# Weight loads of a fused linear-attention and MLP kernel issued from ScalarE's queue instead of SyncE's

## The chip, the cores and the metric

The kernel runs on one core of one Trainium2 chip. Its metric is the device time of one execution in microseconds. Before the change five runs gave a median of 189.07 us (188.53 to 190.00).

A core has TensorE (PE in the profile; its weight loads are PEld), VectorE (DVE), ScalarE (ACT), GpSimd (POOL) and SyncE (SP). Transfers between the chip's main memory and a core's memory are carried by 16 DMA engines. An instruction on SP, ACT or POOL issues such a transfer; "SPq" and "ACTq" in the profile are those engines' instruction streams as far as they issue or wait.

## What is computed

A gated linear attention over 4 batches, 8 heads, 768 steps and head size 48, and then an MLP with SiLU on its 3072 x 384 result:

```python
f = 1.0 / (1.0 + np.exp(-f_logit))
state = np.zeros((B, H, D, D), dtype=np.float32)
for t in range(S):
    state = f[:, :, t, :, None] * state + np.einsum('bhd,bhe->bhde', k[:, :, t], v[:, :, t])
    y[:, :, t] = np.einsum('bhd,bhde->bhe', q[:, :, t], state)
x = y.transpose(0, 2, 1, 3).reshape(B * S, H * D)
h = x @ w_in                       # 384 x 2048
g = h * (1.0 / (1.0 + np.exp(-h)))
out = g @ w_out                    # 2048 x 384
```

All inputs and the output are float32 in main memory. The products run in bfloat16.

## The kernel before

The sequence is cut into 6 chunks of 128 steps; a chunk of one batch is a **unit**, so there are 24 units (unit u has chunk u // 4 and batch u % 4). Two neighbouring units are a pair. For one unit the kernel does the following:

- SP loads f, k, q and v (L485). Units 0 to 3 are loaded singly (192 KB each tensor), the later ones by pairs (384 KB). Each tensor has five tiles that hold a pair each.
- ACT takes an exponential of f (L492) and a logarithm of one plus it (L494). TensorE sums the logs over the chunk with a triangular matrix (`cs`, L565 and L569). ACT takes three exponentials of the sums (`ia` L572, `a` L574, `al` L576).
- POOL multiplies k (L578) and copies v to bfloat16 (L580); DVE multiplies q (L582). TensorE transposes both (`tq`, L588), DVE copies the result out (L590), TensorE makes the scores (`sc`, L599), DVE masks them (L603), TensorE makes the unit's y (L608, L612), DVE casts it (L616), and it is transposed into `xT` (L620, L622). The state is carried on by TensorE (L630), DVE (L635, L637) and POOL (L641). From unit 12 on, the DMA transpose of SP does the first transposition (L592), from unit 15 also the second (L625).
- The MLP: TensorE multiplies by w_in (L529 for units 0 to 5, singly; L540 by pairs) into three PSUM tiles `mlp`, ACT applies SiLU (L526, L536) into `hT`, TensorE multiplies by w_out (L551), DVE copies the result out (L554 to L559) and POOL or SP stores it (L562).

ACT needs one function table for the exponentials and logarithms and another for SiLU. It changes between them with a table load (L677).

**The weights.** w_in and w_out come in four pieces of 768 KB each. A piece is read as float32 into a staging tile and cast to bfloat16 into a tile that stays (L520 on POOL and DVE, L519 on ACT). There are four staging tiles `ws` for w_in (128 x 3 x 512) and two, `wt`, for w_out (128 x 4 x 384), so pieces 3 and 2 of w_out reuse the tiles of pieces 1 and 0 and wait for their casts. The order of the reads is w_in 1, 2, w_out 1, w_in 3, 0, w_out 0, 3, 2. Casts: w_in 0, 1, 2 and w_out 0, 3 on POOL, w_in 3 and w_out 1 on DVE, w_out 2 on ACT. All eight reads are issued by SP among the loads of f, k, q and v (L505, L510).

**The order.** No scheduler on the chip decides anything. A planner in the same file (`make_tasks`, `schedule`, `planned`) gives each task an engine, a duration and a priority, plays the program through with a model of the engines and of the DMA queue, and hands back all tasks sorted by their planned start. `emit` is then called for each in this order, and every engine runs its instructions in the order in which they were emitted. An instruction that has to wait holds up all later ones of its engine. The framework adds the waits that the data demand. It also gives each DMA one of eight semaphores; a DMA's issue waits until the previous DMA with its semaphore has landed.

Before 60 us of planned time, TensorE's idle stretches are filled with products of a blank tile (`warm`, L652).

Of the kernel before, what the change touches and what calls it, by code (L numbers as in the profile page):

```python
# [414 lines left out]
def kernel(  # L415
# [10 lines left out]
    nc = tc.nc  # L426
# [4 lines left out]
    d_model, d_ff = moe_w_in.shape  # L431
# [14 lines left out]
        ws=([128, KT, d_ff // CFG["w_pieces"][0]], F32), wt=([128, NT // CFG["w_pieces"][1], d_model], F32),  # L446
# [12 lines left out]
    NI, NO = CFG["w_pieces"]  # L459
    w_in_sb = [sb.tile([128, KT, d_ff // NI], BF16, name=f"w_in{n}") for n in range(NI)]  # L460
    w_out_sb = [sb.tile([128, NT // NO, d_model], BF16, name=f"w_out{n}") for n in range(NO)]
    w_in_src = moe_w_in.rearrange("(ko ki) n -> ki ko n", ki=128)
# [12 lines left out]
    where = {}  # L475
    for t in tasks:
        for x in t.acq + t.use:
            where[x.key] = buf[x.cls, x.slot]
    at = lambda *key: where[key]

    def load(x, us):
# [14 lines left out]
    def emit(t):  # L496
# [5 lines left out]
        if kind == "wi":  # L502
            w = d_ff // NI
            n = rest[0] * w
            return nc.sync.dma_start(out=at("ws", rest[0]), in_=w_in_src[:, :, n:n + w])  # L505
        if kind == "wo":
            m, w = rest[0], NT // NO
            src = moe_w_out[m * w * 128:(m + 1) * w * 128].rearrange("(m p r) d -> p m r d", p=128, r=4)
            dst = at("wt", m).rearrange("p (m r) d -> p m r d", r=4)
            return nc.sync.dma_start(out=dst[:, 0] if w == 4 else dst, in_=src[:, 0] if w == 4 else src)  # L510
        if kind in ("ci", "co"):
            j, N = rest[0], NI if kind == "ci" else NO
            n, i = divmod(j, 4 // N)
            if kind == "ci":
                dst, src = w_in_sb[n][:, :, 512 * i:512 * i + 512], at("ws", n)[:, :, 512 * i:512 * i + 512]
            else:
                dst, src = w_out_sb[n][:, 4 * i:4 * i + 4, :], at("wt", n)[:, 4 * i:4 * i + 4, :]
# [14 lines left out]
        if kind in ("mi", "si"):  # L532
# [4 lines left out]
            for i in range(2):  # L537
                n = 2 * j + i
# [52 lines left out]
        elif kind == "qkD":  # L591
            nc.sync.dma_start_transpose(out=at("qkT", u).rearrange("p j n c -> p (j n) c"),  # L592
                                        in_=at("qk", u).rearrange("p j h d -> p (j h d)"))
# [60 lines left out]
    with tc.manual_schedule():  # L654
        nc.scalar.preload_act_table_set(SETS[mode])
        blank = sb.tile([C, C], BF16, name="blank")
        nc.vector.memset(blank, 0.0)  # L657
        first = [t for t in tasks if t.eng == "SP"][:4]
        for t in first:
            emit(t)  # L660
        make_upper_triangular(nc, triu, 1.0, diag=True)
        nc.vector.memset(ones, 1.0)
        for cls in ("lf", "qk"):
            for s in range(SLOTS[cls]):
                nc.vector.memset(buf[cls, s][:, :, :, D:64], 0.0)
        make_identity(nc, ident)
        for b in range(B):
            nc.vector.memset(buf[f"st{b}", 0], 0.0)
        acts = [t for t in tasks if t.mode]
        after = {a.idx: b.mode for a, b in zip(acts, acts[1:]) if b.mode != a.mode}  # L670
        for t in tasks:
            while idles and idles[0][0] <= t.start:
                warm(*idles.pop(0)[1:])
            if t not in first:
                emit(t)
            if t.idx in after:
                nc.scalar.preload_act_table_set(SETS[after[t.idx]])  # L677
# [30 lines left out]
```

## Time and profile before

| | us |
|---|---|
| median of five runs | 189.07 |
| the profiled execution | 189.16 |
| its span, first to last instruction | 187.40 |
| TensorE busy in the span | 173.4 |
| ACT busy | 131.2 |
| DVE busy | 95.8 |
| POOL busy | 69.8 |
| blank products (L652) within TensorE's time | 10.0 |

The 16 DMA engines move 34.2 MB, 31.8 MB of them on SP's queue, which takes 78.1% of the 16 engines' span. The TensorE clock was granted in full throughout. Of TensorE's 14.0 idle us, 9.0 lie in the first 30.2 us, 1.1 between 80 and 120 us and 3.8 in the last 9.

How to read it: a row of a timeline has the start, the length, the engine, the line, the operation, output and input tiles with their shapes, the number of instructions merged into the row, and in brackets the idle time of the engine before the row with what ended it. A digit in the row of slices is a tenth of busy time in one fortieth of the span. An engine's idle time matters only where the engine sets the pace.

### The profile page before, as it was taken

Reading aid. Unit: us, or ns where it says so; the run is one execution under the profiler, and the core shown is the slowest. Engines: PE = TensorE matmul, PEld = TensorE weight load, DVE = VectorE, ACT = ScalarE, POOL = GpSimd, SP = SyncE. Lnnn points to the kernel's source line nnn. Section 1 sums busy time; section 2 is a strip of 40 time slices with the busy share of each in tenths; the row PEclk is TensorE's granted clock in tenths of the full one; section 3 lists DMA queues with packets and bytes.
Section 4 is the critical chain, followed back from the end, with each engine's and each line's share of the span. In section 5 each row is a group of like instructions: output and inputs, shape, how many; then the busy total and the mean of one; then the engine's idle time right before and its main releaser. Section 6 shows DMA issues by size and latency. Waiting matters only on the chain.

```text
span 187.4 us, 4875 instructions
## 1 busy us (share of the span) xinstructions
PE 173.4 (93%) x2005; PEld 138.4 (74%) x2005; DVE 95.8 (51%) x185; ACT 131.2 (70%) x217; POOL 69.8 (37%) x112
## 2 busy tenths in 40 slices
PE   5986848999999999979999999999999999999991
PEld 4974747777878889768787787678688886966960
DVE  4287445444877773564627736875542415261011
ACT  4462734998797898998988788668669996810810
POOL 2347528444637470562751642490252006000000
PEclk9999999999999999999999999999999999999999
DMA  6999999899999998999998599478774866413101
GB/s 131 212 176 329 386 353 329 244 226 211 228 207 239 234 214 198 229 251 195 198 167 187 124 179 210 79 122 222 160 149 120 182 121 135 102 25 105 42 17 67
DMA packets 120389, 34.22 MB, mean 183 GB/s; under 512 B 116128, under 2 KB 117792, under 8 KB 120368
## 3 DMA queue, kind: packets, MB, share of 16 engines
q1 hardware_dynamic: 119664, 31.76, 78.1%
q0 software_dynamic: 704, 2.16, 3.3%
q8 instruction: 15, 0.25, 0.6%
q14 instruction: 6, 0.05, 0.1%
HBM read 25.17 MB, written 4.72 MB: 159 GB/s over the span
## 4 chain that ended last, share of the span: by engine, by line
PE 70%; SPq 11%; DMA 7%; ACT 5%; issue 2%; POOL 1%; DVE 1%; DVEq 0%; ACTq 0%
PE mlp L551 29%; PE mlp L540 24%; DMA q<-in_q_dram 7%; SPq L485 7%; SPq L505 4%; PE mlp L529 4%; PE sc L599 3%; PE yd L612 2%; PE yd L608 2%; PE cs L565 2%; ACT L677 2%; PE tq L588 1%; PE yd L630 1%; ACT hT L536 1%; PE tq L620 1%
## 5 line engine op out<-in xcount | busy, mean ns | idle before, releaser
L551 PE MATMUL mlp<-w_out,hT 128*128 128x384 bf16 x384 | 69.9, 326 | 0.0
L536 ACT ACTIVATE hT<-mlp 128x512 bf16<-128x512 f32 x72 | 41.7, 597 | 17.4 <-PE mlp L540 14.9
L540 PE MATMUL mlp<-xT,w_in 128*128 128x256 bf16 x432 | 51.5, 273 | 1.1 <-ACT hT L536 1.0
L551 PEld LDWEIGHTS <-hT 128*128 128x128 bf16 x384 | 34.8, 97 | 19.5
L540 PEld LDWEIGHTS <-w_in 128*128 128x128 bf16 x432 | 46.3, 114 | 3.2 <-issue 1.3
L578 POOL TENSOR_TENSOR qk<-k,ia 128x384 bf16<-128x384 f32 x24 | 24.0, 1001 | 51.9 <-ACT al L576 30.4
L603 DVE TENSOR_TENSOR atm<-sc,triu 128x512 bf16<-128x512 f32 x48 | 30.9, 685 | 19.3 <-PE sc L599 19.3
L677 ACT ACT_TABLE_LOAD x23 | 29.5, 1283 | 0.4
L641 POOL TENSOR_TENSOR st<-sd,al 48x192 bf16<-48x192 f32 x40 | 20.2, 504 | 16.1 <-DVE sd L635 8.6
L529 PE MATMUL mlp<-xT,w_in 128*128 128x128 bf16 x288 | 18.7, 220 | 3.4 <-DVE w_in L520 2.6
L572 ACT ACTIVATE ia<-cs 128x384 f32<-128x384 f32 x24 | 11.8, 490 | 13.9 <-PE cs L569 8.9
L559 DVE COPY o<-mlp 128x384 f32<-128x384 f32 x22 | 12.2, 556 | 18.0 <-PE mlp L551 13.3
L616 DVE CAST yb<-yd 128x384 bf16<-128x384 f32 x24 | 13.3, 553 | 15.8 <-PE yd L612 15.8
L582 DVE TENSOR_TENSOR qk<-q,cs 128x384 bf16<-128x384 f32 x24 | 13.2, 550 | 13.2 <-ACT cs L574 8.4
L529 PEld LDWEIGHTS <-w_in 128*128 128x128 bf16 x288 | 16.8, 114 | 4.2 <-DVE w_in L520 2.8
L526 ACT ACTIVATE hT<-mlp 128x512 bf16<-128x512 f32 x24 | 13.6, 597 | 7.6 <-PE mlp L529 7.2
L580 POOL CAST vb<-v 128x384 bf16<-128x384 f32 x24 | 11.6, 505 | 10.8 <-DMA v<-in_v_dram 10.7
L492 ACT ACTIVATE e<-f 128x768 f32<-128x768 f32 (+1 forms) x14 | 10.5, 748 | 6.7 <-DMA f<-in_f_logit_dram 6.7
L635 DVE TENSOR_TENSOR sd<-yd,st 128x384 f32<-128x384 f32 x16 | 8.9, 554 | 8.3 <-PE yd L630 6.2
L574 ACT ACTIVATE cs<-cs 128x384 f32<-128x384 f32 x24 | 11.4, 477 | 0.6
L652 PE MATMUL mlp<-blank 128*128 128x128 bf16 x112 | 10.0, 256 | 1.0 <-DVE blank L657 1.0
L494 ACT ACTIVATE lf<-e 128x768 bf16<-128x768 f32 (+1 forms) x14 | 10.5, 750 | 0.3
(43 smaller groups left out, 148.6 us busy)
## 6 DMA issues: line engine op xcount, KB each, us to landing
f<-in_f_logit_dram SPq DMA_DIRECT2D x10, 384.0 KB, 5.4
k<-in_k_dram SPq DMA_DIRECT2D x10, 384.0 KB, 5.9
q<-in_q_dram SPq DMA_DIRECT2D x10, 384.0 KB, 5.8
v<-in_v_dram SPq DMA_DIRECT2D x10, 384.0 KB, 5.3
ws<-in_moe_w_in_dram SPq DMA_DIRECT2D x4, 768.0 KB, 8.8
wt<-in_moe_w_out_dram SPq DMA_DIRECT2D x4, 768.0 KB, 8.0
out_dram<-o SPq DMA_DIRECT2D x13, 192.0 KB, 2.1
out_dram<-o POOLq DMA_DIRECT2D x11, 192.0 KB, 3.7
```

The costliest lines, as they stand in the source:

```text
L485: nc.sync.dma_start(out=dst, in_=SRC[x].rearrange("b h s d -> s (b h) d")[c * C:(c + 1) * C, b * H:(b + n) * H])
L526: return nc.scalar.activation(at("hT", P)[:, 4 * j:4 * j + 4, i * C:(i + 1) * C], h, AF.Silu)
L529: nc.tensor.matmul(h[:, r, :], w_tile(kk, 4 * j + r), at("xT", P)[:, kk, i * C:(i + 1) * C], start=(kk == 0), stop=(kk == KT - 1))
L536: return nc.scalar.activation(at("hT", P)[:, 2 * j:2 * j + 2, :], h, AF.Silu)
L540: nc.tensor.matmul(h[:, i, :], w_tile(kk, n), at("xT", P)[:, kk, :], start=(kk == 0), stop=(kk == KT - 1))
L551: nc.tensor.matmul(o, at("hT", P)[:, n, i * C:(i + 1) * C], w_rows(n), start=(n % (NT // 2 if half else NT) == 0), stop=(n == NT - 1 or ha ...
L578: nc.gpsimd.tensor_mul(at("qk", u)[:, 1, :, 0:D], at("k", P)[:, i], at("ia", u))
L582: nc.vector.tensor_mul(at("qk", u)[:, 0, :, 0:D], at("q", P)[:, i], at("cs", u)[:, 0:HD].rearrange("p (h d) -> p h d", d=D))
L603: nc.vector.tensor_mul(at("atm", u)[:, r], at("sc", u)[:, r], triu[:, None, :].to_broadcast([C, NP, C]))
L616: nc.vector.tensor_copy(at("yb", u), at("y", u))
L641: nc.gpsimd.tensor_mul(at("st", u)[lo:lo + D, :, r * D:(r + 1) * D], at("sd", u)[lo:lo + D, :, r * D:(r + 1) * D], at("al", u)[lo:lo + D, ...
L677: nc.scalar.preload_act_table_set(SETS[after[t.idx]])
```

## The change

```diff
     for t in tasks:
         for x in t.acq + t.use:
             where[x.key] = buf[x.cls, x.slot]
+    for n in range(2, NO):
+        where["wt", n] = where["ws", n - 2].rearrange("p k n -> p (k n)").rearrange("p (n d) -> p n d", d=d_model)
     at = lambda *key: where[key]
...
         if kind == "wi":
             w = d_ff // NI
             n = rest[0] * w
-            return nc.sync.dma_start(out=at("ws", rest[0]), in_=w_in_src[:, :, n:n + w])
+            return nc.scalar.dma_start(out=at("ws", rest[0]), in_=w_in_src[:, :, n:n + w])
         if kind == "wo":
             m, w = rest[0], NT // NO
             src = moe_w_out[m * w * 128:(m + 1) * w * 128].rearrange("(m p r) d -> p m r d", p=128, r=4)
             dst = at("wt", m).rearrange("p (m r) d -> p m r d", r=4)
-            return nc.sync.dma_start(out=dst[:, 0] if w == 4 else dst, in_=src[:, 0] if w == 4 else src)
+            return nc.scalar.dma_start(out=dst[:, 0] if w == 4 else dst, in_=src[:, 0] if w == 4 else src)
```

The eight weight pieces are issued by ACT on its own queue. Pieces 2 and 3 of w_out are read into the staging tiles of w_in pieces 0 and 1 (same size, seen in another shape) and wait for the casts of those.

The planner is left as it is: it still counts the weight reads as work of SP, and its order of tasks does not change. In the built program ACT's stream has the eight issues at these places: after unit 2's exponential of f (L492); two after unit 2's last exponential (L574); one between unit 3's exponential and logarithm of f (w_in piece 3); one after unit 3's exponentials and the table load that follows (w_in piece 0); one after the second SiLU (w_out 0), one after the fourth (w_out 3), one after the tenth (w_out 2). SP's stream is the old one without them. On TensorE, DVE and POOL every instruction stands where it stood; only the DMA semaphores that some wait for are others.

## The prediction

> **What bounds the kernel now.** I read the page first (shares, chain of waits), then tables of stretches, then the timelines of SP, ACT, POOL and TensorE over the first 45 us.
>
> ```profile
> PE 70%; SPq 11%; DMA 7%; ACT 5%; issue 2%; POOL 1%; DVE 1%; DVEq 0%; ACTq 0%
> ...
> 19.50:30.20 10.70, 6.41 (x114) 5.92 (x111) 5.27 (x8) 6.12 (x11) 4.91 (x5) 1.00 1.06 376
> 30.20:42.00 11.80, 11.67 (x154) 9.11 (x152) 5.26 (x10) 10.08 (x15) 6.41 (x8) 1.00 1.05 242
> 42.00:80.00 38.00, 38.00 (x509) 31.00 (x506) 25.46 (x49) 33.14 (x56) 18.96 (x32) 1.00 1.07 220
> ```
>
> The columns of a stretch are its length, then the busy time of PE, PEld, DVE, ACT and POOL, the clock, the DMA share and GB/s. The reader is to see two regimes. From 30.2 us TensorE has no room: whatever delays it at 30 us comes out at the end, one for one. Before that it (and through it the 11% of SPq in the chain) waits for data: TensorE idles, 4.3 us of 10.7 between 19.5 and 30.2, while the DMA engines are full (share 1.06). So the change is priced by when TensorE becomes dense. That is decided by a fixed order of work on TensorE and by the order in which loads and weights land:
>
> ```profile
> 18.84 0.32 PE L565 MATMUL cs<-lf,triu 128*128 128x384 bf16 x1 [1.31 <-ACT lf L494]
> ...
> 26.28 0.86 PE L529 MATMUL mlp<-xT,w_in 128*128 128x128 bf16 x12 [2.60 <-DVE w_in L520]
> ...
> 29.73 0.62 PE L588 MATMUL tq<-ident,qk 128*128 128x128 bf16 x8 [0.90 <-DVE qk L582]
> 30.19 1.50 PE L529 MATMUL mlp<-xT,w_in 128*128 128x128 bf16 x24
> ...
> 28.26 1.46 POOL L520 CAST w_in<-ws 128x1536 bf16<-128x1536 f32 x1 [1.02 <-DMA ws<-in_moe_w_in_dram]
> ...
> 17.72 0.52 ACT L492 ACTIVATE e<-f 128x384 f32<-128x384 f32 x1 [3.66 <-DMA f<-in_f_logit_dram]
> ```
>
> In brackets is the idle time before the row and what ended it. cs at 18.84 is unit 3's and hangs on its f load (ACT at 17.72). The 24 products at 30.19 are the first with w_in piece 0 (I call them G); its cast ends at 29.72. SP's own rows show how the weights are woven in:
>
> ```profile
> 10.79 1.96 SPq L505 DMA_DIRECT2D ws<-in_moe_w_in_dram  x1
> 12.79 0.49 SPq L485 DMA_DIRECT2D f<-in_f_logit_dram  x1
> ...
> 32.86 0.44 SPq L510 DMA_DIRECT2D wt<-in_moe_w_out_dram  x1
> ...
> SPq L510 <- DMA wt<-in_moe_w_out_dram: 2.8, 1, 2.8
> SPq L510 <- POOL w_out L520: 1.9, 1, 1.9
> ...
> 13.00:14.00 1.00, 1.00 (x19) 0.79 (x19) 1.00 (x3) 0.97 (x3) 0.50 (x1) 1.00 0.49 59
> 33.00:34.00 1.00, 1.00 (x22) 1.00 (x20) 0.35 (x1) 0.93 (x2) 1.00 (x1) 1.00 0.42 81
> ```
>
> SP stands 4.7 us (28.1 to 32.86) behind the last w_out piece, which waits for its tile; k, q and v of units 4 and 5 stand behind it. Yet the DMA engines ran empty for only 0.51 and 0.58 us (shares 0.49 and 0.42): the queue held enough.
>
> **What the Trainium skill says.** "DMA: Bandwidth & Descriptors", section "Issuing engines are not separate DMA queues": DMAs issued from SP, ACT and GpSimd end on the same 16 engines and interleave; more issuers save only issue time. So bytes do not get faster, only their order changes. Its section "Queues, rings and completion order" says that SP and ACT own one ring each on every engine, and that an engine takes turns between rings, a packet at a time. The trace of before has no second ring of this sort; its nearest case is GpSimd's stores, whose three packets on an engine follow each other without a gap (50.439, 50.625 and 50.811 us, 0.178 us each but the last) although SP's loads were under way. So a turn may be larger than a packet, and how weights and loads share is the unknown here.
>
> **The change part by part.** The built program shows no change of order on TensorE, DVE and POOL; only ACT gains eight issues and SP loses them.
>
> *Amounts.* From 2 to 12 us only loads moved, at 195 to 242, mean 215 GB/s: a load of 192 KB costs 0.92 us of all engines. From 18 to 23 us it was weights at about 394: a piece of 768 KB costs 2.0 us. From issue to first bytes I estimate 1.2 us (the first load, issued at 0.74, moved 15 GB/s in the second 1 to 2), from last byte to landing 0.8 us (traffic ebbs at 13.4, the last load landed at 14.3).
>
> *SP.* It loses 12.3 us of weight issues (1.96 to 4.45 us each where the queue was full) and the waits of 4.7 us. Unit 3's f is issued at 10.8 instead of 12.8, its k, q and v right behind. SP then runs ahead; loads for units 4 to 9 have free tiles. Gain by itself: the two empty DMA stretches, 1.1 us at most.
>
> *w_out pieces 2 and 3 into the w_in tiles.* Their wait is now for the cast of w_in piece 0 or 1, done at 29.7 and 18.4, instead of w_out's at 32.8 and 23.6. On ACT both stand behind silus that themselves need those w_in casts, so these waits cost 0.
>
> *ACT.* Eight issues. The cheapest on SP took 0.35 to 0.6 us, the dearest 4.45; bounds for eight: 3.6 and 12.3 us. I take 0.5 each where the queue is fresh, 1 us once where it is not. Behind the first (11.4 us) waits unit 2's log, +0.5, covered by TensorE's warm-up products and 0.9 us of DVE work. Issues 2 and 3 stand in the 3.66 us ACT waits for unit 3's f: 0. Number 3 also waits for unit 2's v (DMA semaphores are shared by SP and ACT). Issue 4 stands between exp and log of unit 3: 0.5 on the chain. Issue 5, w_in piece 0, stands behind unit 3's exps and the table load. Issues 6 and 7 stand between silus that free the three PSUM tiles of TensorE; 8 ahead of the two silus before unit 4's exp, whose path has 0.6 us (log ends 37.8, cs at 38.4).
>
> *The chain that decides.* If f of unit 3 lands at F: exp 0.55, issue 0.5, log 0.55, cs on TensorE 0.6, three exps 1.1, table 1.3: piece 0 is issued at F + 4.6; first bytes 1.2, transfer 2.0, landing 0.8: F + 8.6; POOL's cast 1.5: G can run at F + 10.1. Now it runs at 30.19, so F may be 20.1, against 17.7 now. What is F? At 12.6, when the first weight piece can flow, about 1.0 us of unit 2's loads is left, then f's own 0.92. Weights taking four fifths of the engines: piece one runs 12.6 to 15.1, loads get 0.5; alone till 15.7 (second piece issued at 14.5), +0.6; second piece till 18.2, +0.5; the rest, 0.3, beside the third piece takes 1.5: f ends at 19.7, F = 20.5. G comes at 30.6; piece 0 too must share, 2.0/0.8 = 2.5, +0.5: 31.1; one stalled issue of 1 us on ACT, half of it in the 1.2 us in which the transfer starts up: +0.5. G at about 31.5, 1.3 us late. Unit 3's k and q, landed by then, do not matter. Nothing takes it back, since TensorE is full from there. Span 188.7, profiled time 190.5 (1.76 us lie around the span); on the median, which is 0.09 below the profiled 189.16: 190.4.
>
> **The rivals.**
> *Loads share evenly* (turns of equal bytes or time): then five pieces, 10 us of traffic, need 20: piece 0 lands at 12.6 + 20 + 0.8 = 33.4 and not at 28.2, G at 34.9; the last three end at 45.4, ACT's cast (1.46) at 46.9, where TensorE asks for that piece at 40.0. That is +4.7 to +6.8, I take 6: 195.1. For it: SP now runs ahead with loads nobody needs yet. Against: the stores' unbroken packets.
> *No change*: with turns of one load against one piece (rest of q to 12.9, piece to 14.9, v to 15.6, piece to 17.6, f to 18.5) F is 19.3, and piece 0 lands at F + 8.6 = 27.9 or part of a turn later, as now (28.2): 189.0. For it: F has 2.4 us of room. Against: the room is narrow. With weights at 0.65 of the engines five pieces take 15.4 us and land at 28.8, 0.6 late; with 0.8 f starves as in the forecast.
> *Faster*: SP is never blocked, both empty stretches are filled (1.1 us) and the 2.6 and 0.9 us waits ahead of G shrink by as much: 187.9. It decides if F stays below 19 and piece 0 lands before 27.2. For it: all bytes up to unit 3's q then fit earlier. Against: ACT issues piece 0 only after F + 4.6, where SP did so at 16.8.
>
> **How the numbers follow.** Chances: the forecast 0.42 (0.10 of it within half a per cent), even sharing 0.20, no change 0.20, faster 0.18 (0.14 beyond half a per cent). About 0.5%, 0.95 us, is what a measurement of this kernel can tell from none. Slower 0.32 + 0.20 = 0.52; same 0.10 + 0.20 + 0.04 = 0.34; faster 0.14. The forecast's own range is 189.3 to 192 (issues from 0.35 us, or several stalled). The whole range goes from 187.8, just under the faster case, to 195.3, the middle of even sharing; what lies outside is under 0.2.
>
> **What would show it.** Unit 3's first exp on ACT later than 17.7, near 20; the issue of w_in piece 0 on ACT near 25; G near 31.5; from there the chain on TensorE as before. It would be wrong if that exp comes before 17.7 while weight casts come 3 us or more late (even sharing), if ACT's issues take far over 0.5 us, or if G comes before 29.5.

## The result, and the profile after

| | before | after |
|---|---|---|
| median of all executions, us | 189.52 (79, from 187.99 to 191.55) | 191.25 (44, from 188.64 to 195.90) |
| ratio to before | 1 | 1.0046, 95% interval 1.0027 to 1.0066 |
| the profiled execution, us | 189.16 | 191.55 |
| its span, us | 187.4 | 189.8 |
| mean granted TensorE clock in it | 1.000 | 0.988 |

The change made the kernel slower, by 0.5% in the ratio and by 0.9% in the medians of all executions. The ratio leaves out executions more than 1.5% above the fastest of their kernel, 21 of the 44 here; all 21 had a mean clock of 0.990 or less, so the ratio understates the change, and medians of all executions stand beside ratios below.

The page of the changed kernel, whose line numbers are higher by two. In the row PEclk a digit is the granted clock in tenths of full speed in a fortieth of the span.

```profile
PEclk9999996999999999999999999999999999999998
...
q1 hardware_dynamic: 117488, 25.47, 67.0%
q10 hardware_dynamic: 2176, 6.29, 8.8%
...
PE 69%; DMA 11%; ACT 7%; SPq 5%; POOL 2%; issue 2%; DVE 1%; ACTq 0%; DVEq 0%
```

The weights have a queue of their own (q10, 6.29 MB); SPq falls from 11% to 5% of the chain, and DMA and ACT take its place. The 6 in the clock's row is what the prediction did not look for. The table of stretches of the changed kernel (columns as in the prediction; the clock is third from the end) puts it in time:

```profile
27.00:28.00 1.00, 0.88 (x16) 0.88 (x17) 0.53 (x2) 0.00 (x0) 0.00 (x0) 1.00 1.00 382
28.00:29.00 1.00, 1.00 (x15) 1.00 (x13) 0.81 (x2) 0.60 (x1) 0.49 (x1) 0.59 0.95 353
29.00:30.00 1.00, 1.00 (x13) 1.00 (x12) 0.32 (x2) 0.60 (x1) 0.97 (x1) 0.50 1.40 329
30.00:31.00 1.00, 1.00 (x13) 1.00 (x11) 0.25 (x1) 0.09 (x1) 0.60 (x2) 0.50 0.92 347
31.00:32.00 1.00, 1.00 (x15) 1.00 (x14) 0.23 (x1) 0.51 (x1) 0.94 (x2) 0.70 0.92 355
```

From 28.19 to 31.60 us, 3.41 us, TensorE had half its clock. Its timeline shows what came before and what it cost:

```profile
27.12 0.86 PE L531 MATMUL mlp<-xT,w_in 128*128 128x128 bf16 x12 [3.20 <-DVE w_in L522]
...
29.40 1.48 PE L531 MATMUL mlp<-xT,w_in 128*128 128x128 bf16 x12
30.67 1.06 PE L590 MATMUL tq<-ident,qk 128*128 128x128 bf16 x8
31.52 1.55 PE L531 MATMUL mlp<-xT,w_in 128*128 128x128 bf16 x24
...
41.87 1.46 PE L553 MATMUL mlp<-w_out,hT 128*128 128x384 bf16 x8 [0.28 <-ACT w_out L521]
...
44.74 1.44 PE L531 MATMUL mlp<-xT,w_in 128*128 128x128 bf16 x23 [0.45 <-ACT hT L528]
```

The same rows before, as far as the prediction doesn't show them:

```profile
27.99 0.83 PE L529 MATMUL mlp<-xT,w_in 128*128 128x128 bf16 x12
...
40.04 1.46 PE L551 MATMUL mlp<-w_out,hT 128*128 128x384 bf16 x8
...
42.34 1.50 PE L529 MATMUL mlp<-xT,w_in 128*128 128x128 bf16 x24
```

The wait for w_in piece 3 grew from 2.60 to 3.20 us, and the first products with it moved from 26.28 to 27.12. Of the rows behind it, the twelve products at 29.40 take 1.48 us, where they took 0.83 before. G, the first products with w_in piece 0, stands at 31.52 and not at 30.19. Further down two waits are new, 0.28 us for ACT's cast of the last w_out piece and 0.45 us for a SiLU behind that cast. These two rows stood at 40.04 and 42.34 before, so they are 1.83 and 2.40 us late, and 2.40 us is the whole difference of the spans.

ACT's timeline in the changed kernel (ACTq are its DMA issues):

```profile
10.85 0.52 ACT L494 ACTIVATE e<-f 128x384 f32<-128x384 f32 x1 [0.48 <-DMA f<-in_f_logit_dram]
10.85 0.50 ACTq L507 DMA_DIRECT2D ws<-in_moe_w_in_dram  x1
11.40 0.52 ACT L496 ACTIVATE lf<-e 128x384 bf16<-128x384 f32 x1
...
17.85 0.52 ACT L494 ACTIVATE e<-f 128x384 f32<-128x384 f32 x1 [3.84 <-DMA f<-in_f_logit_dram]
17.86 0.37 ACTq L507 DMA_DIRECT2D ws<-in_moe_w_in_dram  x1
...
20.51 0.38 ACTq L507 DMA_DIRECT2D ws<-in_moe_w_in_dram  x1
...
34.29 0.33 ACTq L512 DMA_DIRECT2D ws<-in_moe_w_out_dram  x1
...
40.34 1.48 ACT L521 CAST w_out<-ws 128x1536 bf16<-128x1536 f32 x1 [1.14 <-DMA ws<-in_moe_w_out_dram]
```

An issue takes 0.33 to 0.50 us and runs beside the activation that precedes it in the program: unit 2's log starts at 11.40, where it started at 11.44 before. Unit 3's f landed in time (17.83; 17.69 before). The last piece, issued at 34.29 behind ten SiLUs, landed at 40.3; SP had issued it at 32.86, and it landed at 37.5. The issue at 20.51 is that of w_in piece 0. In the trace it has the same semaphore as w_in piece 2, which landed at 20.48. In all eight traces in which ACT issues w_in, piece 0 is issued 0.02 to 0.04 us after piece 2 has landed, so this landing released it.

### The profile page after: what moved, and what is told of

It reads as the page before. It is cut to its first block, busy times and chain, and to the rows that moved or that the text cites. A ratio compares the mean times of both kernels' runs of the same rounds, so it can differ in the third digit from the quotient of the medians.

```text
span 189.8 us, 4877 instructions
## 1 busy us (share of the span) xinstructions
PE 175.2 (92%) x2005; PEld 140.1 (74%) x2005; DVE 95.9 (51%) x185; ACT 131.3 (69%) x217; POOL 70.4 (37%) x112
## 2 busy tenths in 40 slices
DMA packets 120389, 34.22 MB, mean 180 GB/s; under 512 B 116128, under 2 KB 117792, under 8 KB 120368
## 3 DMA queue, kind: packets, MB, share of 16 engines
q10 hardware_dynamic: 2176, 6.29, 8.8%
## 4 chain that ended last, share of the span: by engine, by line
PE 69%; DMA 11%; ACT 7%; SPq 5%; POOL 2%; issue 2%; DVE 1%; ACTq 0%; DVEq 0%
PE mlp L553 29%; PE mlp L542 24%; SPq L487 5%; PE mlp L531 5%; DMA ws<-in_moe_w_in_dram 4%; DMA f<-in_f_logit_dram 4%; PE sc L601 3%; DMA ws<-in_moe_w_out_dram 3%; ACT L679 2%; PE yd L614 2%; PE yd L610 2%; POOL w_out L522 1%; PE cs L567 1%; PE yd L632 1%; PE tq L590 1%
## 5 line engine op out<-in xcount | busy, mean ns | idle before, releaser
L542 PEld LDWEIGHTS <-w_in 128*128 128x128 bf16 x432 | 46.3, 114 | 3.2 <-issue 1.3
L580 POOL TENSOR_TENSOR qk<-k,ia 128x384 bf16<-128x384 f32 x24 | 24.6, 1025 | 53.6 <-ACT al L578 33.7
L643 POOL TENSOR_TENSOR st<-sd,al 48x192 bf16<-48x192 f32 x40 | 20.2, 504 | 17.5 <-DVE sd L637 8.6
L531 PE MATMUL mlp<-xT,w_in 128*128 128x128 bf16 x288 | 19.8, 226 | 4.5 <-DVE w_in L522 3.2
L531 PEld LDWEIGHTS <-w_in 128*128 128x128 bf16 x288 | 17.9, 117 | 5.4 <-DVE w_in L522 3.4
L574 ACT ACTIVATE ia<-cs 128x384 f32<-128x384 f32 x24 | 11.8, 490 | 13.7 <-PE cs L571 9.0
L592 DVE COPY qkT<-tq 128x1024 bf16<-128x1024 bf16 x12 | 8.3, 688 | 4.9 <-PE tq L590 4.9
```

The lines of the kernel that those rows point to most:

```text
L531: nc.tensor.matmul(h[:, r, :], w_tile(kk, 4 * j + r), at("xT", P)[:, kk, i * C:(i + 1) * C], start=(kk == 0), stop=(kk == KT - 1))
L542: nc.tensor.matmul(h[:, i, :], w_tile(kk, n), at("xT", P)[:, kk, :], start=(kk == 0), stop=(kk == KT - 1))
L580: nc.gpsimd.tensor_mul(at("qk", u)[:, 1, :, 0:D], at("k", P)[:, i], at("ia", u))
L643: nc.gpsimd.tensor_mul(at("st", u)[lo:lo + D, :, r * D:(r + 1) * D], at("sd", u)[lo:lo + D, :, r * D:(r + 1) * D], at("al", u)[lo:lo + D, ...
```

## The experiments

The first theory: most of the cost is the clock, which the longer idle stretch of TensorE lost (**clock**). The rival: weights land late, TensorE follows, and the clock only accompanies it (**lateness**). What is left beside the clock I put at first on the last w_out piece. For each kernel I also counted executions whose mean clock was under 0.994. One window of 3.41 us at half clock takes 0.009 from the mean of 189 us, so these have at least one; the idle tail after the last product takes at most 0.004 in the traces. Before: 23 of 59 executions (share 0.39), with a median of 189.34 us for the other 36. After: 36 of 44 (0.82); medians 189.47 without (8), 191.07 between 0.985 and 0.994 (21), 192.11 below (15).

**Keeping TensorE busy in the changed kernel.**

```diff
+            if kind == "m1" and (u, j) == (0, 3):
+                for _ in range(36):
+                    nc.tensor.matmul(h[:, 0, :], blank, blank, start=True, stop=True, skip_group_check=True)
```

> The changed kernel with 36 blank products on TensorE just ahead of the first products with w_in piece 3, inside the idle stretch of 3.2 us (23.9 to 27.1). Clock theory (most of the change's cost is the granted clock, halved for 3.4 us after that stretch): no halved clock at 28 us, about 1.4 us less than the changed kernel in such a run, median near 189.6, ratio to before 0.998 to 1.003. Lateness theory (the weights land late and TensorE simply follows): the median stays near 191.1.

Median 190.26 us, ratio 1.0028 (1.0008 to 1.0047) to a before of 189.69; share of low clock 0.09 instead of 0.82. TensorE in this run:

```profile
23.91 2.17 PE L529 MATMUL mlp<-blank 128*128 128x128 bf16 x36
27.40 0.86 PE L534 MATMUL mlp<-xT,w_in 128*128 128x128 bf16 x12 [1.31 <-DVE w_in L522]
...
30.29 1.53 PE L534 MATMUL mlp<-xT,w_in 128*128 128x128 bf16 x24
...
40.63 1.46 PE L556 MATMUL mlp<-w_out,hT 128*128 128x384 bf16 x8 [0.29 <-ACT w_out L521]
...
43.50 1.50 PE L534 MATMUL mlp<-xT,w_in 128*128 128x128 bf16 x24 [0.45 <-ACT hT L531]
```

w_in piece 3 came even later than in the changed kernel (products at 27.40), and yet G stands at 30.29, where it stood before. So the late weights alone cost 0.1 us up to G. From the first row with piece 3 to G it is 2.89 us here and was 4.40 in the changed kernel: the half clock cost 1.5 us. In the medians the blank products took back 1.0 of the 1.7 us. Lateness, as the main cause, falls. It has a part in it, though: before, this stretch took 3.91 us, 0.90 of them spent waiting for unit 3's q, and as the late piece used up that room, the half clock came out at G almost in full.

But the two later waits of 0.29 and 0.45 us are there, and 0.6 to 0.8 us remain to before (190.26 against 189.69, or 190.10 against 189.34 in executions that kept the clock): the 189.6 that I expected was too low. What this rest is stays open. The eight executions of the changed kernel that kept their clock show 0.1 us of it (189.47 against 189.34), but they are too few to tell 0.1 from 0.8.

**The same blank products in the kernel before.**

> The kernel before with the same 36 blank products in its idle stretch of 2.6 us (23.7 to 26.3). Clock theory: before loses the clock seldom, so little to win, median within 0.5 us of before, with a narrower spread. Lateness theory: no difference at all, or slightly slower.

189.61 us against 189.69, ratio 1.0009 (0.9988 to 1.0030); share of low clock 0.18 against 0.39. As the clock theory has it, there is little to win, and nothing that these executions can tell from zero. That the blank products cost something themselves isn't ruled out either: in executions that kept the clock the median is 189.61 us with them (18) and 189.34 without (36).

**Lengthening the idle stretch in the kernel before.**

```diff
+            if (kind, j) == ("ci", 3):
+                nc.vector.tensor_copy(dst, src)
             return (nc.vector if t.eng == "DVE" else nc.gpsimd).tensor_copy(dst, src)
```

> The kernel before, in which DVE casts w_in piece 3 twice, so that TensorE's idle stretch ahead of it grows by 0.95 us, to about 3.5. Nothing else moves. Clock theory: the share of runs with a mean clock under 0.994 rises from 0.39 to 0.8 or more, and the median by 0.8 to 1.5 us. Lateness theory: TensorE has a wait of 0.9 us for unit 3's q behind it that swallows the delay; 0 to 0.2 us slower, share of clock as before.

191.81 us against 189.82, ratio 1.0125 (1.0078 to 1.0173), share of low clock 1.0 (6 executions). DVE of this run:

```profile
25.62 0.96 DVE L521 CAST w_in<-ws 128x1536 bf16<-128x1536 f32 x1 [2.69 <-DMA ws<-in_moe_w_in_dram]
26.61 1.75 DVE L522 CAST w_in<-ws 128x1536 bf16<-128x1536 f32 x1
```

The second cast took 1.75 us here and not 0.96, so the stretch grew to 5.0 us, more than I had meant; the delay is too large for a clean price. G came at 32.58, 2.4 us late. From the first products with piece 3 to G it took 4.16 us against the 2.89 at full clock above, so by this estimate 1.3 us are the half clock and 1.1 the late cast. The clock went in all six executions.

**Long stretch and blank products together.**

> The kernel before with the double cast of w_in piece 3, which made the idle stretch 5 us and the time 191.8, plus the 36 blank products in that stretch. Clock theory: the delay of 2.1 us at TensorE stays, but the share of low clock falls from 1.0 to under 0.3 and the median by 0.8 us or more (190.2 to 191.0). Lateness theory: 191.5 to 192.

189.81 us against 189.32, ratio 1.0019 (0.9996 to 1.0041); share of low clock 0.45, more than I had set. Of the 2.0 us that the double cast had cost 0.5 are left, less than I had set. This doesn't show that the idle stretch was three quarters of the price, because the late cast was to stay and in the profiled execution it didn't:

```profile
24.68 0.96 DVE L521 CAST w_in<-ws 128x1536 bf16<-128x1536 f32 x1 [1.15 <-DMA ws<-in_moe_w_in_dram]
25.68 0.96 DVE L522 CAST w_in<-ws 128x1536 bf16<-128x1536 f32 x1
```

Piece 3 landed early, at 24.7, the second cast took 0.96 us, and the first products with the piece stood at 26.70 and not at 28.42. What can be said is that within this kernel the 12 executions that kept the clock have a median of 189.58 us and the 10 others 191.20.

**The two parts of the change alone**, the new staging tiles with all issues on SP, and the issues on ACT with the old tiles:

> One part of the change alone: the last two w_out pieces go to the first two w_in staging tiles, all issues stay on SP. SP's standstill ends at the cast of w_in piece 0 (29.8) and not at 32.86, the empty stretch of the DMA engines at 33 us goes. Both theories: 0 to 0.6 us faster than before, since TensorE is dense from 30.2; no halved clock, because w_in piece 3 lands as before at 25.2.

> The other part alone: the eight pieces issued by ACT, w_out pieces 2 and 3 in their old two tiles. Both theories: w_in piece 3 lands near 26.1 as in the changed kernel, so the halved clock is there too, and the last w_out piece, which waits for an earlier cast either way, is issued behind the same silu near 34.3: the time of the changed kernel within 0.4 us (near 191).

Tiles alone: 189.81 us, ratio 1.0012 (0.9990 to 1.0034). SP came to the last piece at 30.4 instead of 32.86, and nothing came of it: the issue took 3.5 us, and the piece landed at 38.1 in the profiled execution, no sooner than the 37.5 of before. The gain I expected isn't there. Nor was the clock safe, contrary to what I had written: it was low in 0.50 of the executions, and in the profiled one, with w_in piece 3 at 25.9 and a stretch of 3.0 us, halved from 27.3 us on. Issues on ACT alone: 191.54, ratio 1.0123 (1.0077 to 1.0169), low clock in 5 of 6, w_in piece 3 landed at 26.3, the last w_out piece at 40.3. This is the changed kernel again, as far as six executions tell: the cost is that of the issues, the tiles are neutral.

**w_in back on SP, w_out on ACT.**

```diff
-            return nc.scalar.dma_start(out=at("ws", rest[0]), in_=w_in_src[:, :, n:n + w])
+            return nc.sync.dma_start(out=at("ws", rest[0]), in_=w_in_src[:, :, n:n + w])
```

> w_in's four pieces issued by SP as before, w_out's four by ACT with the changed tiles. Theory that SP's loads running ahead take turns from w_in piece 3: here it stands in SP's own queue ahead of unit 3's k, lands by 25.5, share of low clock as in before (0.4), median 189.5 to 190.4 (the last w_out piece is still issued late behind a silu). Theory that any weight traffic on a second queue does it: w_in piece 3 lands at 26 or later, share 0.8, median near 191.

190.16 us against 189.82, ratio 1.0001 (0.9975 to 1.0026). w_in piece 3 landed at 24.4, so in SP's own queue it isn't pushed back: that part held. One trace alone would prove little, since the landing varies, but over all of them piece 3 landed at 24.4 to 26.0 us where SP issues w_in (six traces) and at 25.9 to 27.4 where ACT does (eight). The share of low clock did not fall, it was 0.91, and the trace suggests why:

```profile
24.01 1.47 PE L531 MATMUL mlp<-xT,w_in 128*128 128x128 bf16 x12 [2.67 <-POOL w_in L522]
25.28 0.52 PE L614 MATMUL yd<-vb,atm 128*128 128x48 bf16 x8
25.63 1.42 PE L531 MATMUL mlp<-xT,w_in 128*128 128x128 bf16 x12
26.88 0.29 PE L654 MATMUL mlp<-blank 128*128 128x128 bf16 x2
27.00 0.83 PE L531 MATMUL mlp<-xT,w_in 128*128 128x128 bf16 x12
```

Now w_out piece 1, on ACT's queue, took its turns beside w_in piece 2, which landed at 22.4 and not at 20.2. The idle stretch of 2.67 us moved ahead of piece 2, and the half clock with it (23.5 to 26.9). It cost less there: G came at 29.80, ahead of before, since piece 3 and unit 3's loads were in hand behind it. So a half clock costs less where TensorE would have waited soon after anyway.

**The last w_out piece earlier.** Five kernels were to test the rest. Two moved its issue three SiLUs ahead, without and with the blank products:

```diff
+            if t.name == ("m1", 0, 0):
+                emit(*[x for x in tasks if x.name == ("wo", 2)])
-            if t not in first:
+            if t not in first and t.name != ("wo", 2):
                 emit(t)
```

> The changed kernel with the issue of the last w_out piece three silus earlier in ACT's stream (31.5 and not 34.3 us). Theory that what is left beside the clock is this piece's landing (ACT's cast waits 1.1 us for it, TensorE 0.3 and then 0.45 us): piece lands by 38, the waits go, 0.6 to 1.0 us faster than the changed kernel (190.3 to 190.7), share of low clock still 0.8. Rival (the rest is spread over ACT and DMA): within 0.3 us of the changed kernel.

> Both: the early issue of the last piece and the 36 blank products. If clock and last piece are the two terms of the change's cost, this comes to 189.3 to 189.7, ratio to before 0.997 to 1.001, share of low clock 0.1 or less. If something else remains, it stays near 190.2 as with the blank products alone.

201.80 and 201.21 us, ratios 1.0634 and 1.0603. Both expectations fell for a reason of their own. ACT of the first:

```profile
41.48 0.33 ACTq L512 DMA_DIRECT2D ws<-in_moe_w_out_dram  x1
41.86 1.57 ACT L528 ACTIVATE hT<-mlp 128x512 bf16<-128x512 f32 x3 [11.74 <-DMA f<-in_f_logit_dram]
```

Moved to another place in the order of emission, the issue was given another of the eight DMA semaphores, last held by SP's load of f for units 6 and 7. That landed at 41.4, and ACT stood 11.7 us. A third kernel put the piece into the tile of w_in piece 2, free since 22 us, and issued it right behind the piece before it, with the blank products:

```diff
-        where["wt", n] = where["ws", n - 2].rearrange(...)
+        where["wt", n] = where["ws", 2 if n == 2 else 1].rearrange(...)
...
+            if t.name == ("wo", 3):
+                emit(*[x for x in tasks if x.name == ("wo", 2)])
```

> The changed kernel with two things: the last w_out piece goes to the staging tile of w_in piece 2 (free since 22 us) and is issued by ACT right after the piece before it (26.5 to 27.6 us, not 34.3), and the 36 blank products. If the late landing of this piece is the term that the blank products left (0.3 and 0.45 us of TensorE waits, 0.76 us over before in runs with the clock kept): it lands by 36, ACT's cast doesn't wait, median 189.3 to 189.8, ratio to before 0.997 to 1.002. If something else remains: 190.1 or more.

201.79 us, ratio 1.0632: the same trap with the semaphore of v of units 4 and 5.

```profile
26.22 13.59 ACTq L512 DMA_DIRECT2D ws<-in_moe_w_out_dram  x2
39.85 1.57 ACT L531 ACTIVATE hT<-mlp 128x512 bf16<-128x512 f32 x3 [15.36 <-DMA v<-in_v_dram]
```

The other two let POOL issue it, which touches no semaphore of SP or ACT:

```diff
-            return nc.scalar.dma_start(out=dst[:, 0] if w == 4 else dst, ...)
+            return (nc.gpsimd if m == 2 else nc.scalar).dma_start(out=dst[:, 0] if w == 4 else dst, ...)
```

> The changed kernel, in which POOL and not ACT issues the last w_out piece, right after its cast of w_out piece 0 (near 32 us; ACT did it at 34.3). No DMA semaphore of ACT or SP changes. Theory that the rest of the cost is this piece's landing: it lands by 38, TensorE's waits of 0.3 and 0.45 us behind it go, 0.5 to 1.0 us faster than the changed kernel (190.3 to 190.8), share of low clock about 0.8 as there. Rival (the rest is spread): within 0.3 us of the changed kernel.

> The same with the 36 blank products. If clock and last piece are the two terms of the cost: 189.3 to 189.8, ratio to before 0.997 to 1.001, share of low clock 0.1. If something else remains, near 190.2, as with the blank products alone.

191.77 us (1.0127, 1.0092 to 1.0162) and 190.46 us (1.0062, 1.0040 to 1.0085). POOL got to the issue only at 34.1 and 34.3 us, behind its cast of w_out piece 0, and the piece landed at 39.9 and 40.2: not moved, so neither speaks for or against. The pair repeats the first experiment, though: blank products take the share of low clock from 6 of 6 to 0.32 and 1.3 us from the time. In the profiled execution of the second one w_in piece 0 landed at 30.3 with the clock kept, G came at 31.84, and the execution took 191.53 us: lateness does cost where it passes the slack ahead of G.

## Why the prediction was right, and where

The direction, the size and the range held: 190.4 was forecast, +1.3 us; the ratio makes it +0.9, the medians of all executions +1.7. The road was another one, so the size is in good part luck. Of the signs that the prediction named in advance G near 31.5 came, but unit 3's first exp came at 17.85 and not near 20, and w_in piece 0 was issued at 20.51 and not near 25.

*From 30.2 us TensorE is full, what delays it there comes out at the end.* Held: +1.33 us at G (31.52; I had 31.5), +1.38 at the products at 40.08 (38.70 before). The rest of the 2.4 us in the span came later, behind the last w_out piece.

*The chain that decides, F + 10.1.* Failed, though it gave G to 0.1 us. F was put at 20.5 because f was to starve behind the second piece; f landed at 17.83. Weights took about the share that I set while a piece flowed: 0.79 of the engines' time and over nine tenths of the bytes from 13 to 15 us. The packets came almost one for one there, 297 of 2 KB against 284 of 192 B, and again from 22 to 23 us, 156 against 156. That fits turns of one packet each, as the prediction quotes them; its doubt, drawn from the stores, is not borne out. But between the first piece and the second the loads had the engines nearly to themselves, 1127 packets against 21 from 15.5 to 16.5 us, and in these f came through. In the sum the term "piece, rest, piece, rest" was mis-sized by 2.7 us.

Piece 0 was issued at F + 2.7, not F + 4.6. It waited neither for the issues before it nor for the table load (which starts at 20.56), but for the landing of piece 2, whose semaphore it shares. From issue to landing it then took 7.9 us, where the sum had 4.5 with the sharing. So one error took back most of the other: it landed at 28.45, 0.24 us later than before, and its cast ended at 29.96. G at 31.52 didn't wait for it, TensorE was still at half clock with the work ahead of G. That both roads end at 31.5 (the sum's own terms give 31.6) is chance.

*ACT's issues, 0.5 us each on the chain and one stalled.* Failed: 0.33 to 0.50 us each, beside the activation ahead of them, and none on the chain. The trace of before had no ACT issue; a price of zero was the bound I didn't take. The Trainium skill says (DMA: Bandwidth & Descriptors, "Issuing engines are not separate DMA queues") that issuing on several engines at once "will only save the time on the sequencer it takes to initiate the DMA". This case agrees: the same 34.22 MB moved at a mean of 183 GB/s before and 180 GB/s after. What changed is the order of the landings.

*What made G late in their place.* w_in piece 3, which I had left out of the chain, landed at 26.08 instead of 25.24, since loads that used to stand behind it in SP's queue now took their turns ahead of it (unit 3's k landed at 20.75 instead of 26.07). By itself that cost 0.1 us up to G, as the blank products showed. It made an idle stretch of 3.20 us, after which the clock was halved for 3.41 us on a full TensorE. The Trainium skill describes this gate (TensorE: Matmul & The Clock Gate, "Part 1: The HAM clock gate (the "warmup" mystery)"): a free-running window of about 3.4 us, half clock after an idle one. The length agrees to 0.01 us, and the 20.48 us of full clock ahead of 28.19 are six such windows. That the window must be idle doesn't agree: if it was the 3.41 us before 28.19, it held 1.07 us of products. I had the stretch of 2.60 us on the page and treated idle time as if it cost only itself.

*The last piece.* The prediction weighed its issue only by what it could hold up on ACT, 0.6 us of room ahead of unit 4's sums, and that room held (the log ends at 39.20, cs starts at 39.81). The piece itself it put at nothing, and that failed: issued 1.4 us later than before, it landed 2.8 us later, and in the profiled execution the waits of 0.28 and 0.45 us behind it and what they shift make the 1.07 us between G and 44.74. They appear in the first experiment too, with the clock kept. That an earlier issue takes them away was not shown, since in none of the five kernels it landed by 38 us, as was meant.

*The rivals.* Even sharing would have put piece 0 at 33.4; it landed at 28.45. Faster asked for F below 19, which came, and for piece 0 before 27.2, which didn't; SP stood 11.3 us in one issue of k (21.11 to 32.45), where it had stood 4.7 us for a tile. By the landings "no change" came closest, with F well inside its room and piece 0 landing about as before, and it is what the changed kernel does in the 8 executions of 44 that kept their clock: 189.47. It missed the clock, as the forecast did.

## What to carry to other kernels

Idle time of TensorE isn't free to grow even where it stays under 3.41 us, the time for which the clock was halved here. A piece that came 0.84 us later cost 1.33 us at G with the half clock behind it, and 0.1 us with 36 blank products in the stretch; in the medians these products took back 1.0 us. So read an idle stretch ahead of a full TensorE for what it does to the clock, and try filling it.

Moving transfers to a second queue moved the turns and not the bytes, so ask which transfer that stood behind now goes ahead. Where DMA semaphores are few and shared between issuing engines, one issue moved in the program can wait for another engine's latest load, or for an earlier one of its own: look at the waits of the built program before running it.

## What the runs showed that was not expected

- The clock is a lottery: the same program ran with none, one or more half-clock windows. The kernel before had at least one in 39% of executions, which its single profiled execution, with a mean clock of 1.000, doesn't show. With w_out on ACT it was 91%, and the profiled execution had only 2.67 us of idle time ahead of its half clock.
- A DMA issue on ACT starts with the activation ahead of it (10.85 and 10.85 us) and doesn't delay the next one.
- One issue can hold its engine for long: 11.34 us on SP for one 384 KB load, with 0.33 to 0.50 us on ACT's queue at the same time. That SP's queue was full is likely, since unit 3's q and v and the f ahead of this load landed only at 27.6, 32.7 and 34.0, but no run shows how much a queue takes.
- A second cast of the same 128 x 1536 tile on DVE took 1.75 us directly behind one of 0.96 us in one execution, and 0.96 us in another. Why is open.
